# An attention and feed-forward kernel: batch 3 by casting loads, two tails earlier, one load by head pairs

## The chip, the cores and the metric

The kernel runs on one core of one Trainium2 chip. Times are microseconds (us) on the device, medians of several executions. A ratio is the mean time of one kernel's fast runs over the mean of the other kernel's fast runs of the same rounds, so it is not quite the ratio of the medians quoted beside it. The first run of the kernel before, 1282.54 us, is left out.

Engines: PE is TensorE, which multiplies matrices; DVE is VectorE; ACT is ScalarE; POOL is GpSimd; SP is SyncE, which here only issues DMAs. A name ending in q (SPq) is an engine's queue: the time that an issue took there, waits included where the queue could not go on.

## The reference

```python
# both functions are condensed
def _attn_ref(q, k, v):                  # 8 batches, 8 heads, 576 rows, 64 columns, float32
    scores = (1 / np.sqrt(D)) * np.matmul(q, k.transpose(0, 1, 3, 2))
    scores = np.where(block_i >= block_j, scores, -1e9)      # blocks of 64 rows, causal
    attn = np.exp(scores - scores.max(-1, keepdims=True))
    attn = attn / (attn.sum(-1, keepdims=True) + 1e-9)
    return np.matmul(attn, v)

# x: the heads side by side, 4608 x 512; w_gate, w_val: 512 x 1536; w_out: 1536 x 512
def _moe_ref(x, w_gate, w_val, w_out):
    return (np.maximum(x @ w_gate, 0) * (x @ w_val)) @ w_out
```

## The kernel before

The feed-forward part works through nine tiles of 512 rows. Tile j < 8 is rows 0 to 511 of batch j; the ninth gathers the 64 last rows ("tails") of every batch. A tile is 144 products of 128x512 on PE: 96 for gate and val, 48 for the output. The attention of later batches is put between these products by hand: an event `(p, f)` runs `f` after product `p` of the tile. The attention of a batch is four rounds of two heads each (rounds 8 to 11 are batch 2, round 12 is the first of batch 3), and one tail.

```python
def round_at(p, r, av, to_xT, after=(6, 13)):
    # scores and exponentials of round r at p, products with v at av,
    # and then to_xT(r): its result, transposed, into the tile xT of its batch
    ...

def to_xT_dma(r):                                # by a DMA that SP issues
    b, hp = divmod(r, 4)
    nc.sync.dma_start_transpose(xT_of(b)[:, hp, :]..., xnats[r]...)

def to_xT_pe(r, evac):                           # by PE, used for batches 0 and 1
    ...
    for c in range(4):
        nc.tensor.transpose(br[:, 128 * c : 128 * c + 128], xnat[:, c, :], ident)
    evac(xT_of(b)[:, hp, :], br[:, 0:512])
```

Batches get to the chip in two ways. Batches 0 to 3 are loaded as float32 into a staging buffer by SP and cast by POOL, DVE or ACT. Batches 0 and 1 are then transposed by PE, batches 2 and 3 by DMAs, whose results DVE and POOL put into order ("unpermute"). Batches 4 to 7 take casting loads: POOL issues a DMA that turns float32 into bfloat16 on its way, 15 loads for a batch, and SP issues four transposes from SBUF to SBUF for q and k.

```python
def load_qkv(b, which):                          # casting loads, issued by POOL
    for t in which:
        for c in range(NCH):                     # 5 chunks of rows
            ...
            nc.gpsimd.dma_start(dst, src[b, :, 128 * c : 128 * c + n, :]...)

def dma_transposes(b):                           # four transposes, issued by SP
    ...
    for t in range(2):
        nc.sync.dma_start_transpose((qTm, kTm)[t][b % 2]..., m[t])
        nc.sync.dma_start_transpose((qTt, kTt)[t][b % 2][:, 0:4, :], tl[t])
```

qTm, kTm, qTt, kTt and v_bf exist twice and are used in turn, so batch b + 2 overwrites batch b. Each engine runs its own program in order and does not wait for PE unless a buffer makes it wait. An event's place therefore fixes only the order on each engine, not the time: POOL and SP run ahead of PE when they can.

The schedule of tile 1, which the change rewrites (... marks a cut):

```python
events = tail_at(24, 0, (40, 44)) + tail_at(116, 1, (132, 136))
for r, p in ((8, 41), (9, 58), (10, 75), (11, 92)):
    events += round_at(p, r, (p + 21, p + 25), (p + 25, to_xT_dma))
events += [
    (88, lambda: e1.pe_tails((dve, act))),
    ...
    (47, load_3),                                # batch 3, staged
    ...
    (66, lambda: mains_3(0)),                    # its casts
    (81, lambda: early[3].transpose(0)),
    (82, lambda: mains_3(4)),
    (101, lambda: early[3].transpose(1)),
    (118, lambda: early[3].transpose_tails()),
    (121, un(3, 0, (dve, pool))),                # its unpermutes
    ...
]
run(144, events)
for b in range(3, B):                            # tile b - 1
    ...
    for at, which in ((4, (0, 1)), (46, (2,))):
        events.append((at, lambda b=b, w=which: load_qkv(b + 1, w)))
    events.append((66, lambda b=b: dma_transposes(b + 1)))
    run(144 * (b - 1), events)
```

The softmax here doesn't subtract the row's maximum and nothing guards it: scores larger than these inputs give would overflow.

Of the kernel before, what the change touches and what calls it, by code (L numbers as in the profile page):

```python
# [17 lines left out]
def kernel(  # L18
# [79 lines left out]
    def new_bf():  # L98
        return [sb.tile([128, 2048], BF, name=n, bufs=2) for n in ("q_bf", "k_bf")]

    def new_bt():
        return [sb.tile([64, 512], BF, name=n, bufs=2) for n in ("q_bt", "k_bt")]
# [161 lines left out]
    def load_qkv(b, which):  # L264
        for t in which:
            src = (q, k, v)[t]
            for c in range(NCH):
                n = 128 if c < 4 else 64
                if t == 2:
                    dst = v_bf[b % 2][:n, c, :, 0:64]  # L270
                else:
                    if (b, 0) not in bfs:
                        bfs[b, 0], bfs[b, 1] = new_bf(), new_bt()
                    dst = bfs[b, 0][t][:, 512 * c : 512 * c + 512] if c < 4 else bfs[b, 1][t]
                    dst = dst.rearrange("p (h d) -> p h d", h=8)
                nc.gpsimd.dma_start(  # L276
                    dst,
                    src[b, :, 128 * c : 128 * c + n, :].rearrange("h p d -> p h d"),
                )
# [3 lines left out]
    def dma_transposes(b):  # L283
        m, tl = bfs[b, 0], bfs[b, 1]
        for t in range(2):
            nc.sync.dma_start_transpose(
                (qTm, kTm)[t][b % 2].rearrange("p c h n -> p (c h) n"),
                m[t],
            )
            nc.sync.dma_start_transpose((qTt, kTt)[t][b % 2][:, 0:4, :], tl[t])  # L290
# [27 lines left out]
    def load_w_out(i):  # L318
        return load_w(wo[i], moe_w_out, 512 * i)

    def cast_w(sts, eng):
        for dst, st in sts:
            eng(dst, st)
# [118 lines left out]
    def corners(r, zero):  # L442

        at = attnT[r % 4]
        for lo, n in ((0, 512), (896, 128)):
            two = at[64:128, :, lo : lo + 2 * n].rearrange("p g (c n) -> p g c n", c=2)
            zero(two[:, :, :, 0:64])
# [36 lines left out]
    def tail_to_xT(b, x):  # L484
        nc.sync.dma_start_transpose(xTt[:, b], x)
# [197 lines left out]
    dve, act, pool = nc.vector.tensor_copy, nc.scalar.copy, nc.gpsimd.tensor_copy  # L683
# [7 lines left out]
    with tc.manual_schedule(engines={E.PE, E.DVE, E.Activation, E.Pool, E.SP}):  # L691

        e0 = Early(0)
# [55 lines left out]
        e1, e2 = Early(1), Early(2)  # L749
# [2 lines left out]
        w_out = [load_w_out(i) for i in range(2)]  # L752
        e1.load_v(0, 4)
        w_out.append(load_w_out(2))
        e1.load_qk(4, 4)
        e1.load_v(4, 4)
        e0.load_tails((0, 1))
        e0.load_tails((2,))
        e2.load_qk(0, 4)
        e2.load_qk(4, 4)  # L760
        for g in range(2):
# [5 lines left out]
        cast_w(w_out[2][:1], pool)  # L767
        last_w = [[a[:, c : c + 1] for a in w_out[2][1]] for c in range(2)]
        cast_w(last_w[:1], pool)
        e1.cast_qk(4, 4, (pool, None))  # L770
        e1.cast_v(4, 4, pool)
        e0.cast_tails((pool, pool))
        e0.cast_v_tail(pool)
        place = [32]

        def upto(p):
# [3 lines left out]
        def run(base, events):  # L780
            for p, f in sorted(events, key=lambda e: e[0]):
                upto(base + int(p))
                f()

        def round_at(p, r, av, to_xT, after=(6, 13)):

            exps = []

            def begin():
                exps.extend(visit(r))  # L790
                exps[0]()
                exps[1]()

            return [
                (p, begin),
                (p + after[0], lambda: exps[2]()),
                (min(p + after[1], av[0] - 0.5), lambda: corners(r, zero_dve)),
                *(
                    [(av[0], lambda: both_av(r))]
                    if av[1] is None  # L800
                    else [(av[i], lambda i=i: head_av(r, i)) for i in range(2)]
                ),
                (to_xT[0], lambda: to_xT[1](r)),
            ]

        def tail_at(p, b, av):
            exps = []
            x = sb.tile([64, 512], BF, name="xtail", bufs=2)

            def begin():  # L810
                exps.extend(tail_visit(b))
                exps[0]()
                exps[1]()

            def end():
                tail_av(b, 1, x)
                tail_to_xT(b, x)

            return [
                (p, begin),  # L820
                (p + 6, lambda: exps[2]()),
                (av[0], lambda: tail_av(b, 0, x)),
                (av[1], end),
            ]
# [4 lines left out]
        early = {2: e2}  # L829

        def tails_2():
            e1.cast_tails((pool, pool))
            e1.cast_v_tail(pool)
            e2.cast_tails((pool, pool))
            e2.transpose_tails()
            e2.cast_v_tail(pool)

        def v_2():
            e2.cast_v_chunks(0, pool)
            e2.cast_v_chunks(1, pool)  # L840

        def load_3():
            e3 = early[3] = Early(3)
            e3.load_qk(0, 4)
            e3.load_tails((0, 1))
            e3.load_qk(4, 4)
            e3.load_tails((2,))
            e3.load_v_chunks(0)
            e3.load_v_chunks(1)

        def mains_3(h0):
            early[3].cast_qk(h0, 4, (pool, pool))
            if h0 == 4:
                early[3].cast_tails((pool, pool))

        def v_3():
            e3 = early[3]
            for g in range(2):
                e3.cast_v_chunks(g, pool)
            e3.cast_v_tail(pool)  # L860

        def un(b, hp, engs=(dve, dve)):
            return lambda: early[b].unpermute(hp, engs)

        def mains_2(h0):
            e2.load_v_chunks(h0 // 4)
            e2.cast_qk(h0, 4, (pool, pool))
            e2.transpose(h0 // 4)

        def load_tails():  # L870
            e1.load_tails((0, 1))
            e1.load_tails((2,))
            e2.load_tails((0, 1))
            e2.load_tails((2,))

        events = round_at(96, 4, (112, 112.1), (116, pe_xT), (6, 11))
        events += round_at(104, 5, (127, 127.1), (131, pe_xT), (6, 15))
        events += round_at(128.5, 6, (139, 140), (146, pe_xT), (4, 9))
        events += round_at(138, 7, (148, None), (153, pe_xT), (3, 8))
        events += [  # L880
            (80, lambda: e1.cast_qk(0, 4, (None, dve))),
            (93, lambda: e1.pe_mains(0, (dve, act))),
            (95, lambda: e1.pe_mains(1, (dve, act))),
            (112.05, lambda: cast_w(last_w[1:], dve)),
            (120.2, lambda: e1.cast_qk(4, 4, (None, act))),
            (123, lambda: e1.pe_mains(2, (dve, act))),
            (125, lambda: e1.pe_mains(3, (dve, act))),
            (128, lambda: mains_2(0)),
            (142, lambda: e0.pe_tails((dve, act))),
            (143, lambda: mains_2(4)),  # L890
            (143, load_tails),
        ]
        run(0, events)
        events = tail_at(24, 0, (40, 44)) + tail_at(116, 1, (132, 136))
        for r, p in ((8, 41), (9, 58), (10, 75), (11, 92)):
            events += round_at(p, r, (p + 21, p + 25), (p + 25, to_xT_dma))
        events += [
            (88, lambda: e1.pe_tails((dve, act))),
            (20, lambda: store.pop()()),
            (25, un(2, 0, (dve, pool))),  # L900
            (28, un(2, 1, (dve, pool))),
            (46, v_2),
            (47, load_3),
            (52, un(2, 2, (dve, pool))),
            (56, un(2, 3, (dve, pool))),
            (60, tails_2),
            (66, lambda: mains_3(0)),
            (81, lambda: early[3].transpose(0)),
            (82, lambda: mains_3(4)),
            (101, lambda: early[3].transpose(1)),  # L910
            (118, lambda: early[3].transpose_tails()),
            (121, un(3, 0, (dve, pool))),
            (125, un(3, 1, (dve, pool))),
            (137, v_3),
        ]
        run(144, events)
        for b in range(3, B):
            events = tail_at(120, b, (136, 140))
            if b == 3:
                events += tail_at(3, 2, (21, 25))  # L920
            for i, p in enumerate((27, 50, 73, 96) if b == 3 else (2, 32, 62, 92)):
                r = 4 * b + i
                events += round_at(p, r, (p + 20, p + 24), (p + 24, to_xT_dma))
            if b == 3:
                events.append((2, un(3, 2, (dve, pool))))
                events.append((40, un(3, 3, (dve, pool))))
            if b + 1 < B:
                for at, which in ((4, (0, 1)), (46, (2,))):
                    events.append((at, lambda b=b, w=which: load_qkv(b + 1, w)))
                events.append((66, lambda b=b: dma_transposes(b + 1)))  # L930
            run(144 * (b - 1), events)
# [30 lines left out]
```

## Time and profile before

| | before |
|---|---|
| time, median of the runs beside the changed kernel | 373.54 us |
| profiled span | 372.0 us |
| PE busy | 96% |
| DVE, ACT, POOL busy | 47%, 46%, 30% |
| longest wait of PE | 3.9 us, at tile 2's start |

The head of the page of the kernel before, with the span and the busy times of the engines:

```profile
span 372.0 us, 7467 instructions
## 1 busy us (share of the span) xinstructions
PE 357.1 (96%) x2963; PEld 176.8 (48%) x2963; DVE 173.4 (47%) x399; ACT 169.5 (46%) x278; POOL 112.9 (30%) x142
```

PE is the limit. What can still be won is its idle time, which the list of PE's waits names (the three longest; total us, number, longest):

```profile
PE ffnp L568 <- DMA xT<-xnat: 3.9, 1, 3.9
PE ffnp L679 <- POOL ident masks.py:199: 1.6, 1, 1.6
PE ffnp L238 <- ACT k_bf L168: 1.6, 1, 1.6
```

L568 is a gate or val product: tile 2's fourth product waits for the xT transpose of round 11, the last of batch 2. L238 is the transposing of batch 1's k on PE, which waits for ACT's cast. The timeline of PE around the first wait (start, us, operation; what ended the idle time stands in brackets):

```profile
109.96 0.38 PE L568 MATMUL ffnp<-xT,wg 128*128 128x512 bf16 x1 [3.91 <-DMA xT<-xnat]
110.18 1.29 PE L568 MATMUL ffnp<-xT,wv 128*128 128x512 bf16 x4
111.26 1.91 PE L568 MATMUL ffnp<-xT,wg 128*128 128x512 bf16 x4
112.97 1.64 PE L568 MATMUL ffnp<-xT,wv 128*128 128x512 bf16 x4
114.45 1.03 PE L568 MATMUL ffnp<-xT,wg 128*128 128x512 bf16 x4
```

A group of four products usually starts 0.86 us after the one before it. After the wait a group takes 1.71 us: the clock is at half. The 13 products from 109.96 to 114.45 took 4.5 us instead of 2.8, so the wait costs 3.9 + 1.7 = 5.6 us. This is what the Trainium skill describes ("TensorE: Matmul & The Clock Gate", Part 1): PE's clock is halved after an idle window of about 3.4 us and comes back after a window as long of work. The trace's clock record agrees with one half-clock stretch of 3.4 us here.

POOL's timeline shows the casting loads of batch 4 and 5 (four lines of it; x4 and x5 are numbers of loads):

```profile
110.87 3.65 POOL L276 DMA_DIRECT2D q_bf<-in_q_dram  x4
120.32 4.54 POOL L276 DMA_DIRECT2D v_bf<-in_v_dram  x5
124.84 3.52 POOL L276 DMA_DIRECT2D q_bf<-in_q_dram  x4
132.47 0.77 POOL L276 DMA_DIRECT2D k_bt<-in_k_dram  x1
```

SP's timeline shows batch 4's four transposes, and behind them the xT transposes:

```profile
127.77 4.88 SPq L286 DMA_TRANSPOSE qTm<-q_bf  x1
132.75 1.26 SPq L290 DMA_TRANSPOSE qTt<-q_bt  x1
134.19 6.70 SPq L286 DMA_TRANSPOSE kTm<-k_bf  x1
140.98 1.20 SPq L290 DMA_TRANSPOSE kTt<-k_bt  x1
142.28 4.62 SPq L543 DMA_TRANSPOSE xT<-xnat  x3
```

Read together: 25 loads leave POOL as one train, and the four transposes issued into it hold SP for 14.4 us (127.8 to 142.2). Batch 5's four, issued from 168.7 us on, when the last of the loads ahead of them was landing (at 169.1 us), took 7.5.

### The profile page before, as it was taken

What the parts mean: (1) busy time and instruction counts of PE and PEld (TensorE: products, weight loads), DVE (VectorE), ACT (ScalarE), POOL (GpSimd) and SP (SyncE); (2) the same over time, 40 slices, a digit from 0 to 9 for tenths busy, and PEclk for the clock granted to TensorE, in tenths of its full rate; (3) what the DMA queues carried; (4) which work ended last, traced back from release to release, by engine and by line L of the source; (5) the groups of instructions that cost most, each with busy time, mean ns of one, the idle gap of its engine ahead of it and who ended that gap; (6) DMA issues with size and microseconds to landing.
All of it is one profiled execution on the core that took longest, in us unless ns stands there. A gap on an engine that the chain in (4) does not pass through costs nothing.

```text
span 372.0 us, 7467 instructions
## 1 busy us (share of the span) xinstructions
PE 357.1 (96%) x2963; PEld 176.8 (48%) x2963; DVE 173.4 (47%) x399; ACT 169.5 (46%) x278; POOL 112.9 (30%) x142
## 2 busy tenths in 40 slices
PE   6899979999959999999999999999999999999996
PEld 2544545544534545444554455444544454444443
DVE  4754465675513553454345543554354543323432
ACT  4833736667234663456435544553465323302310
POOL 5756644385079930750067004000000000000000
PEclk9999999999998999999999999999999999999999
DMA  8999999989889999998499846956210120020014
GB/s 252 289 348 359 306 250 319 206 209 248 132 157 115 126 143 204 116 129 149 114 89 140 123 120 82 62 74 140 79 17 14 52 92 7 0 86 28 0 34 109
DMA packets 145187, 51.35 MB, mean 138 GB/s; under 512 B 124544, under 2 KB 139136, under 8 KB 145152
## 3 DMA queue, kind: packets, MB, share of 16 engines
q1 hardware_dynamic: 83616, 34.62, 43.5%
q0 software_dynamic: 56256, 7.08, 38.6%
q10 hardware_dynamic: 5280, 9.18, 7.7%
q8 instruction: 23, 0.38, 0.5%
q14 instruction: 12, 0.10, 0.1%
HBM read 37.75 MB, written 9.44 MB: 127 GB/s over the span
## 4 chain that ended last, share of the span: by engine, by line
PE 83%; DMA 13%; SPq 1%; ACT 1%; POOL 0%; issue 0%; DVE 0%; ACTq 0%; POOLq 0%
PE ffnp L568 45%; PE ffnp L625 24%; DMA stage<-in_moe_w_gate_dram 5%; PE ffnp L491 4%; DMA stage<-in_k_dram 3%; PE sc L378 3%; PE ffnp L471 3%; DMA stage<-in_moe_w_out_dram 2%; PE one L378 1%; DMA xT<-xnat 1%; SPq L139 1%; DMA stage<-in_v_dram 1%; PE sc L412 1%; PE one L412 0%; ACT gate_sb L578 0%
## 5 line engine op out<-in xcount | busy, mean ns | idle before, releaser
L583 DVE TENSOR_TENSOR hT<-gate_sb,ffnp 128x512 bf16<-128x512 bf16 x106 | 72.8, 687 | 97.5 <-PE ffnp L568 83.2
L578 ACT ACTIVATE gate_sb<-ffnp 128x512 bf16<-128x512 f32 x108 | 64.8, 601 | 106.6 <-PE ffnp L568 103.1
L568 PE MATMUL ffnp<-xT,wg 128*128 128x512 bf16 x384 | 104.3, 382 | 4.8 <-DMA xT<-xnat 3.9
L625 PE MATMUL ffnp<-wo,hT 128*128 128x512 bf16 (+1 forms) x444 | 102.1, 374 | 0.2 <-DVE ob L645 0.2
L568 PE MATMUL ffnp<-xT,wv 128*128 128x512 bf16 x376 | 101.4, 382 | 0.0
L568 PEld LDWEIGHTS <-wv 128*128 128x128 bf16 x432 | 40.1, 98 | 50.3 <-issue 7.4
L568 PEld LDWEIGHTS <-wg 128*128 128x128 bf16 x432 | 40.3, 98 | 48.3 <-issue 5.6
L625 PEld LDWEIGHTS <-hT 128*128 128x128 bf16 x444 | 40.6, 98 | 41.5 <-issue 1.1
L387 ACT ACTIVATE attnT<-sc 128x1024 bf16<-128x1024 f32 x56 | 57.0, 1039 | 0.2 <-issue 0.2
L659 DVE COPY ob<-ffnp 128x512 f32<-128x512 f32 (+1 forms) x35 | 23.7, 677 | 39.1 <-PE ffnp L625 39.1
L276 POOL DMA_DIRECT2D v_bf<-in_v_dram x20 | 17.1, 883 | 69.5 <-PE ffnp L471 69.5
L491 PEld LDWEIGHTS <-attnT 128*128 128x128 bf16 x640 | 26.2, 98 | 13.9 <-DVE xnat L457 3.5
L456 DVE RECIPROCAL recip<-ffnp 128x4 f32<-128x4 f32 (+1 forms) x73 | 13.1, 179 | 33.1 <-PE ffnp L491 21.3
L491 PE MATMUL ffnp<-v_bf,attnT 128*128 128x65 bf16 x570 | 26.4, 194 | 0.0
L393 ACT ACTIVATE attnT<-one 128x256 bf16<-128x256 f32 x28 | 10.7, 383 | 33.1 <-PE ffnp L378 28.3
L457 DVE TENSOR_TENSOR xnat<-ffnp,recip 128x256 bf16<-128x256 f32 x57 | 24.2, 425 | 2.6 <-DMA xT<-xnat 0.7
L433 ACT ACTIVATE attnTt<-one 64x256 bf16<-64x256 f32 x8 | 3.0, 378 | 33.5 <-PE ffnp L412 33.5
L378 PE MATMUL sc<-qTm,kTm 64*128 64x512 bf16 (+1 forms) x168 | 17.4, 305 | 0.0
L378 PEld LDWEIGHTS <-kTm 64*128 64x128 bf16 x224 | 9.6, 94 | 15.0 <-issue 10.7
L424 ACT ACTIVATE attnTt<-sc 128x1024 bf16<-128x1024 f32 x16 | 15.6, 1014 | 0.0
L223 POOL COPY kTm<-perm 128x512 bf16<-128x512 bf16 x8 | 9.7, 1231 | 19.1 <-DMA perm<-k_bf 14.1
L276 POOL DMA_DIRECT2D k_bf<-in_k_dram x16 | 14.3, 953 | 0.0
(87 smaller groups left out, 262.6 us busy)
## 6 DMA issues: line engine op xcount, KB each, us to landing
out_dram<-ob ACTq DMA_DIRECT2D x32, 256.0 KB, 2.5
stage<-in_moe_w_gate_dram SPq DMA_DIRECT2D x6, 512.0 KB, 9.0
stage<-in_moe_w_val_dram SPq DMA_DIRECT2D x6, 512.0 KB, 8.8
stage<-in_q_dram SPq DMA_DIRECT2D x6, 512.0 KB, 6.4
stage<-in_k_dram SPq DMA_DIRECT2D x6, 512.0 KB, 7.5
stage<-in_moe_w_out_dram SPq DMA_DIRECT2D x6, 512.0 KB, 8.5
stage<-in_v_dram SPq DMA_DIRECT2D x20, 128.0 KB, 5.3
stage<-in_v_dram SPq DMA_DIRECT2D x8, 256.0 KB, 6.5
```

Source lines behind the costliest of these rows:

```text
L276: nc.gpsimd.dma_start(dst, src[b, :, 128 * c : 128 * c + n, :].rearrange("h p d -> p h d"),)
L378: nc.tensor.matmul(where[c].rearrange("p (c n) -> p c n", n=128), kTm[b % 2][head_of(hh), c, hp, :], qTm[b % 2][head_of(hh), c:4, hp, :], ...
L387: return lambda: nc.scalar.activation(at[:, :, lo : lo + 512], sc, AF.Exp, scale=scale)
L424: return lambda: nc.scalar.activation(at[:, :, 2 * i : 2 * i + 2, 0:256], main[i].rearrange("p g (h n) -> p g h n", h=2), AF.Exp, scale=scale,
L456: nc.vector.reciprocal(recip, av[:, :, 64])
L457: nc.vector.tensor_tensor(out=out, in0=av[:, :, 0:64], in1=recip.to_broadcast([rows, n, 64]), op=AX.mult,)
L491: nc.tensor.matmul(av[:, p, :], at[:, col : col + 128], v_bf[b % 2][:, c, h, :], start=(p == 0), stop=(c == p), skip_group_check=True,)
L568: nc.tensor.matmul(to, (wg, wv)[t][f // 4][:, c, 128 * (f % 4) : 128 * (f % 4) + 128], x[:, c], start=(c == 0), stop=(c == 3),)
L578: nc.scalar.activation(gate_sb, gate, AF.Relu)
L583: nc.vector.tensor_tensor(out=h, in0=gate_sb, in1=val, op=AX.mult)
L625: nc.tensor.matmul(op, hT[f][:, 128 * s : 128 * (s + 1)], wo[f // 4][:, f % 4, n0:n1], start=(f == lo), stop=(f == hi - 1),)
L659: nc.vector.tensor_copy(ob, op)
```

## The change

The intent: load batch 3 like the later batches, which spares POOL's casts and the unpermutes on DVE and POOL. For that batch 1's buffers must be free earlier, so both tails of batches 0 and 1 go ahead of batch 2's rounds. The second half of batch 1's q and k is loaded and cast two heads at a time, so that PE gets the first pair sooner.

The diff, cut to its core (... marks cuts; what is left out is the removed `load_3`, `mains_3`, `v_3`, the places where batch 1's tails were loaded and cast before and the casts by POOL that go with the moved loads, and batch 2's third unpermute, now at 50 instead of 52):

```diff
-        e1.load_qk(4, 4)
+        for h0 in (4, 6):
+            e1.load_qk(h0, 2)
         e1.load_v(4, 4)
-        e0.load_tails((0, 1))
-        e0.load_tails((2,))
+        for e in (e0, e1):
+            e.load_tails((0, 1))
+            e.load_tails((2,))
         e2.load_qk(0, 4)
 ...
-        events += round_at(128.5, 6, (139, 140), (146, pe_xT), (4, 9))
+        events += round_at(126, 6, (138.2, 139), (146, pe_xT), (4, 9))
 ...
-            (120.2, lambda: e1.cast_qk(4, 4, (None, act))),
+            (119, lambda: e1.cast_qk(4, 2, (None, act))),
+            (120.2, lambda: e1.cast_qk(6, 2, (None, act))),
             (123, lambda: e1.pe_mains(2, (dve, act))),
-            (125, lambda: e1.pe_mains(3, (dve, act))),
+            (129, lambda: e1.pe_mains(3, (dve, act))),
 ...
+            (142, lambda: e1.pe_tails((dve, act))),
 ...
-        events = tail_at(24, 0, (40, 44)) + tail_at(116, 1, (132, 136))
-        for r, p in ((8, 41), (9, 58), (10, 75), (11, 92)):
-            events += round_at(p, r, (p + 21, p + 25), (p + 25, to_xT_dma))
+        events = tail_at(24, 0, (37, 39)) + tail_at(40, 1, (55, 58))
+        for r, p in ((8, 54), (9, 67), (10, 80), (11, 94)):
+            events += round_at(p, r, (p + 21, p + 24), (p + 24, to_xT_dma))
         events += [
-            (88, lambda: e1.pe_tails((dve, act))),
 ...
-            (47, load_3),
-            (60, tails_2),
-            (66, lambda: mains_3(0)),
-            ... (transposes, casts and unpermutes of batch 3)
+            (59, lambda: load_qkv(3, (0, 1))),
+            (90, tails_2),
+            (92, lambda: load_qkv(3, (2,))),
+            (105, lambda: dma_transposes(3)),
         ]
```

At 105 batch 3's four transposes enter SP's queue, and round 11's xT follows at 94 + 24 = 118.

More of the change, by code (lines that the diff above doesn't have):

```diff
@@ L769 @@
         cast_w(last_w[:1], pool)
-        e1.cast_qk(4, 4, (pool, None))
+        for h0 in (4, 6):
+            e1.cast_qk(h0, 2, (pool, None))
         e1.cast_v(4, 4, pool)
-        e0.cast_tails((pool, pool))
-        e0.cast_v_tail(pool)
+        for e in (e0, e1):
+            e.cast_tails((pool, pool))
+            e.cast_v_tail(pool)
         place = [32]
@@ L831, in tails_2 @@
         def tails_2():
-            e1.cast_tails((pool, pool))
-            e1.cast_v_tail(pool)
             e2.cast_tails((pool, pool))
@@ L840, in v_2 @@
             e2.cast_v_chunks(1, pool)
-        def load_3():
-            e3 = early[3] = Early(3)
-            e3.load_qk(0, 4)
-            e3.load_tails((0, 1))
-            e3.load_qk(4, 4)
-            e3.load_tails((2,))
-            e3.load_v_chunks(0)
-            e3.load_v_chunks(1)
-        def mains_3(h0):
-            early[3].cast_qk(h0, 4, (pool, pool))
-            if h0 == 4:
-                early[3].cast_tails((pool, pool))
-        def v_3():
-            e3 = early[3]
-            for g in range(2):
-                e3.cast_v_chunks(g, pool)
-            e3.cast_v_tail(pool)
         def un(b, hp, engs=(dve, dve)):
@@ L870, in load_tails @@
         def load_tails():
-            e1.load_tails((0, 1))
-            e1.load_tails((2,))
             e2.load_tails((0, 1))
@@ L902 @@
             (46, v_2),
-            (47, load_3),
-            (52, un(2, 2, (dve, pool))),
+            (50, un(2, 2, (dve, pool))),
             (56, un(2, 3, (dve, pool))),
-            (60, tails_2),
-            (66, lambda: mains_3(0)),
-            (81, lambda: early[3].transpose(0)),
-            (82, lambda: mains_3(4)),
-            (101, lambda: early[3].transpose(1)),
-            (118, lambda: early[3].transpose_tails()),
-            (121, un(3, 0, (dve, pool))),
-            (125, un(3, 1, (dve, pool))),
-            (137, v_3),
+            (59, lambda: load_qkv(3, (0, 1))),
+            (90, tails_2),
+            (92, lambda: load_qkv(3, (2,))),
+            (105, lambda: dma_transposes(3)),
         ]
@@ L923 @@
                 events += round_at(p, r, (p + 20, p + 24), (p + 24, to_xT_dma))
-            if b == 3:
-                events.append((2, un(3, 2, (dve, pool))))
-                events.append((40, un(3, 3, (dve, pool))))
             if b + 1 < B:
```

## The prediction

> **What bounds the kernel now.** TensorE: busy 357.1 of 372.0 us (busy times of the page). In stretches of 10 us it is busy 10.00 from 110 to 360 us, so only the first third has time to give. PE's waits name it: 3.9 us at 105.8 us, where tile 2's first product waits for batch 2's last xT transpose; 1.6 us at 50.3 us, for the ScalarE cast of batch 1's k; start-up. After the 3.9 us wait, eight matmuls start 0.43 instead of 0.216 us apart, 1.7 us more; the clock record shows half clock for 3.4 us, as the Trainium skill says ("TensorE: Matmul & The Clock Gate", Part 1: half rate after an idle window of about 3.4 us). So this boundary costs 5.6 us.
>
> **What the change does.** PE gets the same work in another order. Removed: batch 3's unpermutes (DVE 0.6, GpSimd about 1.2 us each), GpSimd casts (about 1 us each) and staged loads. DVE and GpSimd are 47% and 30% busy: off the critical path, worth nothing directly.
>
> - *Head pairs.* k of heads 4, 5 lands about 1.5 us before all of k, and its cast is half of 1.05 us. The 1.6 us wait should mostly go. Estimate: -1.3 us.
> - *Tails earlier.* Needed so that batch 3 can overwrite batch 1's buffers. They leave only some 26 matmuls, 6 us, between round 11's transpose (position 118) and tile 2.
> - *Batch 3 by casting loads.* GpSimd takes 0.9 us for each issue and runs ahead: q, k, v of batch 3 and q, k of batch 4 go out as one train of 25 loads. The kernel before has just this train for batches 4 and 5: 110.9 to 133.2 us, the last landing 146.6. The four transposes issued inside it took 14.4 us on SP (127.8 to 142.2; 7.5 us at 168.7, without loads), and the xT transpose behind them landed at 148.3. The skill ("DMA: Bandwidth & Descriptors", Queues, rings and completion order) says why: each DMA engine takes packets from its queues in turn. The DMA share of 2.2 there agrees.
>
> The train should now start when GpSimd is done with batch 2's unpermutes, near 77 us. Batch 3's transposes start near 95.5 us, and **round 11's xT waits behind them on SP**: it lands at 106 us (uncongested) to 115 us (as in the train). PE wants it at about 103 us; before, PE resumed at 109.9. So the wait is not removed: it moves and probably grows, half clock after it included.
>
> **Prediction.** Resumption shifts by -3.5 us (uncongested) to +5 us, weighted to the second; from there PE is packed as before. 377 us, 370 to 383 in 8 of 10. Faster by over 2%: 0.06; within 2%: 0.79; slower by over 2%: 0.15.
>
> **What would show it.** PE's waits: that for the cast of k under 0.6 us; that for xT still the largest, 3 to 12 us, at 102 to 115 us. SP's queue: batch 3's four transposes just ahead of round 11's xT, 7 to 14 us in all. GpSimd: casting loads from about 77 us in one train. Granted clock: half for about 3.4 us after the wait. Windows after that: PE 10.00.
>
> **What would make it wrong.** Transposes done before round 11's product (up to 7 us gained); batch 4's loads held back; a new wait in rounds 8 to 11, now 13 instead of 17 matmuls apart.

## The result

The changed kernel took 384.24 us (383.83 to 384.79, 4 runs) against 373.54 us; the ratio is 1.0298, with a 95% interval of 1.0259 to 1.0336. It is slower by 3%, outside the predicted range of 370 to 383 us.

The head of its page:

```profile
span 382.3 us, 7410 instructions
## 1 busy us (share of the span) xinstructions
PE 354.3 (93%) x2915; PEld 176.5 (46%) x2963; DVE 170.1 (44%) x395; ACT 169.3 (44%) x279; POOL 112.6 (29%) x145
```

The list of PE's waits (the longest, and two that are new):

```profile
PE ffnp L568 <- DMA xT<-xnat: 12.8, 1, 12.8
PE ffnp L625 <- POOL wo L323: 1.5, 1, 1.5
PE ffnp L471 <- DVE hT L583: 1.2, 1, 1.2
```

The same product waits for the same transpose, 12.8 us instead of 3.9. PE's timeline behind it (four lines of it):

```profile
119.78 0.58 PE L568 MATMUL ffnp<-xT,wg 128*128 128x512 bf16 x1 [12.76 <-DMA xT<-xnat]
121.86 1.91 PE L568 MATMUL ffnp<-xT,wg 128*128 128x512 bf16 x4
123.57 1.34 PE L568 MATMUL ffnp<-xT,wv 128*128 128x512 bf16 x4
124.74 1.03 PE L568 MATMUL ffnp<-xT,wg 128*128 128x512 bf16 x4
```

PE goes on at 119.8 us, 9.8 us later than before (109.96). The 13 products to 124.74 (one has no record in the trace) take 5.0 us, 2.2 more than at full clock; before, it was 1.7 more. The later start and the 0.5 us more of half clock sum to 10.3 us, which is the whole difference of the two spans. From there on the lists of waits show nothing of note in either trace.

SP's timeline says why xT is late:

```profile
92.82 5.51 SPq L543 DMA_TRANSPOSE xT<-xnat  x2
98.52 6.71 SPq L286 DMA_TRANSPOSE qTm<-q_bf  x1
105.33 1.23 SPq L290 DMA_TRANSPOSE qTt<-q_bt  x1
106.73 5.93 SPq L286 DMA_TRANSPOSE kTm<-k_bf  x1
112.76 1.21 SPq L290 DMA_TRANSPOSE kTt<-k_bt  x1
114.06 1.22 SPq L543 DMA_TRANSPOSE xT<-xnat  x1
```

Round 11's products with v were done at about 100 us, but SP issued its transpose only at 114.1, when batch 3's four were through: 15.5 us for these (98.5 to 114.0). It landed 5.7 us after its issue. SP did not wait for data of batch 3 here: the last load of its q and k, issued at 88.4 us, had landed by 93.9 us. The four went out right behind round 10's xT, and for that SP had to wait until DVE had made round 10's result from PE's products:

```profile
96.69 0.42 DVE L457 TENSOR_TENSOR xnat<-ffnp,recip 128x256 bf16<-128x256 f32 x1
97.14 1.19 SPq L543 DMA_TRANSPOSE xT<-xnat  x1
```

So PE's own pace set when the four entered the queue. And POOL's timeline shows the train around them (four lines of it):

```profile
80.46 3.86 POOL L276 DMA_DIRECT2D q_bf<-in_q_dram  x4
90.80 4.24 POOL L276 DMA_DIRECT2D v_bf<-in_v_dram  x5
94.95 3.60 POOL L276 DMA_DIRECT2D q_bf<-in_q_dram  x4
103.09 0.69 POOL L276 DMA_DIRECT2D k_bt<-in_k_dram  x1 [0.36 <-issue]
```

The q of batch 3 leaves at 80.5 us; that of batch 4, which no one needs before tile 3, leaves at 95.0, just ahead of the transposes.

### The profile page after: what moved, and what is told of

It is laid out like the page before. It is cut to its first block, busy times and chain, and to the rows that moved or that the text cites. A ratio compares the mean times of both kernels' runs of the same rounds, so it can differ in the third digit from the quotient of the medians.

```text
span 382.3 us, 7410 instructions
## 1 busy us (share of the span) xinstructions
PE 354.3 (93%) x2915; PEld 176.5 (46%) x2963; DVE 170.1 (44%) x395; ACT 169.3 (44%) x279; POOL 112.6 (29%) x145
## 4 chain that ended last, share of the span: by engine, by line
PE 76%; DMA 14%; SPq 6%; issue 1%; POOL 1%; DVE 1%; POOLq 0%
PE ffnp L568 42%; PE ffnp L625 22%; DMA stage<-in_moe_w_gate_dram 5%; PE ffnp L491 4%; SPq L139 4%; PE sc L378 3%; PE ffnp L471 3%; DMA stage<-in_v_dram 2%; DMA stage<-in_k_dram 2%; DMA perm<-q_bf 2%; SPq L286 2%; DMA xT<-xnat 1%; PE one L378 1%; DMA stage<-in_q_dram 1%; SPq L158 1%
## 5 line engine op out<-in xcount | busy, mean ns | idle before, releaser
L568 PE MATMUL ffnp<-xT,wg 128*128 128x512 bf16 x367 | 101.5, 383 | 14.4 <-DMA xT<-xnat 12.8
L625 PE MATMUL ffnp<-wo,hT 128*128 128x512 bf16 (+1 forms) x421 | 98.2, 373 | 3.0 <-POOL wo L323 1.5
L276 POOL DMA_DIRECT2D v_bf<-in_v_dram x25 | 21.0, 866 | 96.7 <-PE ffnp L471 96.7
L276 POOL DMA_DIRECT2D q_bf<-in_q_dram x20 | 18.1, 947 | 0.0
L276 POOL DMA_DIRECT2D k_bf<-in_k_dram x20 | 17.9, 954 | 0.0
L378 PEld LDWEIGHTS <-kTm 64*128 64x128 bf16 x224 | 9.5, 94 | 15.5 <-issue 11.3
```

The costliest lines, as they stand in the source:

```text
L378: nc.tensor.matmul(where[c].rearrange("p (c n) -> p c n", n=128), kTm[b % 2][head_of(hh), c, hp, :], qTm[b % 2][head_of(hh), c:4, hp, :], ...
L568: nc.tensor.matmul(to, (wg, wv)[t][f // 4][:, c, 128 * (f % 4) : 128 * (f % 4) + 128], x[:, c], start=(c == 0), stop=(c == 3),)
L625: nc.tensor.matmul(op, hT[f][:, 128 * s : 128 * (s + 1)], wo[f // 4][:, f % 4, n0:n1], start=(f == lo), stop=(f == hi - 1),)
```

## The experiments

Two theories were set against each other. **Q**: the order on SP holds xT back, since it stands behind the transposes of batch 3. **T**: the train of casting loads makes every transpose slow, whatever the order. A third possibility had to be kept open: that the earlier tails and the denser rounds cost time themselves. The runs came in three groups, each on one chip with its own runs of the kernel before (medians 374.39, 373.85 and 374.10 us). All results were correct.

| run | edit, on which kernel | us | ratio to before | 95% interval |
|---|---|---|---|---|
| a_swap | xT of round 11 ahead of batch 3's transposes, changed | 379.49 | 1.0154 | 1.0091 to 1.0218 |
| a_hold4 | batch 4's loads held back, changed | 375.54 | 1.0043 | 0.9984 to 1.0101 |
| a_pe11 | xT of round 11 by PE, changed | 377.61 | 1.0080 | 1.0005 to 1.0155 |
| b_pe11 | xT of round 11 by PE, before | 373.22 | 0.9961 | 0.9895 to 1.0027 |
| a_pe11_gates | both cures, changed | 370.02 | 0.9907 | 0.9859 to 0.9955 |
| b_pe11_gates | both cures, before | 370.77 | 0.9912 | 0.9874 to 0.9950 |
| c_order | the change without its casting loads | 374.30 | 1.0011 | 0.9961 to 1.0062 |
| a_junk | 54 idle products in the wait, changed | 382.66 | 1.0225 | 1.0171 to 1.0279 |
| a_same | the changed kernel again | 385.11 | 1.0292 | 1.0263 to 1.0322 |
| a_late_tails | batch 1's tails behind batch 2, changed | 382.94 | 1.0242 | 1.0205 to 1.0279 |
| a_junk66 | 66 idle products in the wait, changed | 383.67 | 1.0271 | 1.0238 to 1.0305 |
| b_pairs | the head pairs alone, before | 374.56 | 1.0007 | 0.9981 to 1.0032 |

### a_swap: the other order on SP

```diff
-            (105, lambda: dma_transposes(3)),
+            (119, lambda: dma_transposes(3)),
```

> The changed kernel with batch 3's four transposes issued behind round 11's xT transpose on SP instead of ahead of it. Theory Q (the order on SP holds xT back): xT is issued near 101 us and lands by about 108 us instead of 119.7; PE's wait for it falls from 12.8 to 0 to 1.5 us. Batch 3's own transposes then start 4 us later and land near 122 us, so round 12 (27 matmuls into tile 2) should wait some 6 us: total 377 to 380. Rival theory T (the train of casting loads alone makes xT slow, whatever the order): xT still lands near 119 us and the total stays at 383 to 385.

The list of PE's waits of this run:

```profile
PE one L378 <- DMA kTm<-k_bf: 5.1, 1, 5.1
PE ffnp L568 <- DMA xT<-xnat: 3.1, 1, 3.1
```

The wait for xT fell from 12.8 to 3.1 us, so the order on SP is a cause. It did not fall to 1.5: issued at about 100.6 us, xT still needed 9.3 us to land (PE went on at 109.9), because the train was under way. Both theories hold a part. The four transposes, now later, let round 12 wait 5.1 us for kTm: about half of what the one wait lost, the next one took. The total was 379.49 us.

### a_hold4: batch 4's loads held back

POOL copies one column of tile 2's xT before it issues batch 4's loads. A real read of the data makes it wait, so no race arises. The order on SP is as in the changed kernel.

```diff
+    gate = consts.tile([128, 1], BF, name="gate")
 ...
+                if b == 3:      # ahead of load_qkv(4) in the events of tile 2
+                    events.insert(
+                        0, (4, lambda: nc.gpsimd.tensor_copy(gate, xT_of(2)[:, 3, 0:1])))
```

> The changed kernel with batch 4's casting loads held back: GpSimd first copies one column of tile 2's xT, so they start only when round 11's xT has landed. The order on SP is unchanged. Theory T (the second half of the train makes the four transposes slow): they take 7 to 9 us on SP instead of 15.5, xT lands at 109 to 112 us, PE waits 2 to 5 us, total 374 to 377. Theory Q in its pure form (only the order matters, the train does not): xT lands near 119 us as before, total 383 to 385.

SP's timeline (without the line of qTt), and under it two lines of POOL's, of this run:

```profile
97.87 3.82 SPq L287 DMA_TRANSPOSE qTm<-q_bf  x1
103.16 3.35 SPq L287 DMA_TRANSPOSE kTm<-k_bf  x1
106.62 1.19 SPq L291 DMA_TRANSPOSE kTt<-k_bt  x1
107.90 1.22 SPq L544 DMA_TRANSPOSE xT<-xnat  x1
```

```profile
90.11 4.24 POOL L277 DMA_DIRECT2D v_bf<-in_v_dram  x5
110.39 0.19 POOL L906 COPY gate<-xT 128x1 bf16<-128x1 bf16 x1 [16.04 <-DMA xT<-xnat]
```

The four transposes took 9.9 us instead of 15.5, a little more than expected; batch 3's v was still landing until 100.8 us. xT stood behind them as ever and landed in time for PE to go on at 110.4. The wait was 4.0 us, the total 375.54 us. So pure Q falls: with the order unchanged, taking half of the train away wins back nearly all. The loss needs both, a queue in order and a train that slows what stands ahead in it. By what means the loads slow a transpose inside the DMA engines, no run here isolates.

### a_pe11 and b_pe11: no DMA at the boundary

Round 11's result is transposed by PE, as it is for batches 0 and 1 (for the kernel before, 25 and 31 in place of 24 and 30).

```diff
-            events += round_at(p, r, (p + 21, p + 24), (p + 24, to_xT_dma))
+            to_xT = (p + 24, to_xT_dma) if r < 11 else (p + 30, lambda r: to_xT_pe(r, act))
+            events += round_at(p, r, (p + 21, p + 24), to_xT)
```

> The changed kernel with round 11's xT made by four TensorE transposes and a ScalarE copy, so nothing at the boundary waits for a DMA. Theory Q and T both: the 12.8 us wait is gone. Batch 3's transposes still land at 119 us, so round 12, which PE reaches near 115.5 us, should wait about 4 us: total 374 to 377. If the lost time is elsewhere (the earlier tails, the denser rounds), the total stays above 380.

> The kernel before with the same edit. Its wait of 3.9 us for xT and the 1.7 us of half clock behind it should go, 0.3 us of transposes come: 368 to 369.5 us, 0.985 to 0.989 of before. If the half clock is not caused by the wait, only 3.6 us are won: 370 us.

The longest wait of each, a_pe11 first:

```profile
PE one L378 <- DMA kTm<-k_bf: 6.3, 1, 6.3
```

```profile
PE ffnp L568 <- DMA xT<-xnat: 3.5, 2, 2.5
```

In the changed kernel the wait at the boundary is gone, and round 12 waits 6.3 us for batch 3's kTm instead: 4 us were expected. In the kernel before the boundary is clear as well, but the expected 368 to 369.5 us did not come. The trace shows two new waits for xT, 1.0 and 2.5 us, at 147 to 151 us, at the start of tile 3. PE arrived there earlier, while batch 3's xT transposes stood behind batch 4's four in the train of that time: the one that ended the longer wait was issued 5.1 us earlier than before, at 140.6, and yet landed at 151.2 us, as before (151.1). The gain was taken back one boundary later, by the same mechanism.

### a_pe11_gates and b_pe11_gates: both cures

To the edit above, for every batch from 3 on, a copy that holds back the next batch's loads until the last transpose of this batch has landed:

```diff
+                events.insert(
+                    0, (4, lambda b=b: nc.gpsimd.tensor_copy(gate, kTt[b % 2][:, 0, 0:1])))
```

> The changed kernel with round 11's xT made by TensorE, and from batch 4 on each batch's casting loads held back on GpSimd until the last transpose of the batch before has landed (a copy of one column of kTt). Theory (order on SP and the train of loads together make the whole loss): no wait for xT, and round 12's wait for kTm, 6.3 us with the TensorE transposes alone, goes as well, because batch 3's transposes now land near 109 us; the next boundary stays clear too. PE packed from 20 us on but for 2 to 4 us of small waits: 369 to 371.5 us, 0.985 to 0.992 of before. Rival (the denser rounds or the earlier tails cost by themselves): 375 or more.

> The kernel before with the same two edits. With the TensorE transposes alone it had no wait at tile 2, but 3.5 us of waits for xT at tile 3, behind batch 4's transposes inside the train of loads. If the train is the cause of these too, holding batch 5's loads back removes them and the half clock after them: 367.5 to 370 us, 0.980 to 0.988 of before. If not, the 3.5 us stay: 372 to 374.

The page's line of the granted clock in 40 slices of the span, in tenths, first of the changed kernel, then of a_pe11_gates:

```profile
PEclk9999999999975999999999999999999999999999
```

```profile
PEclk9999999999999999999999999999999999999999
```

What is left of the wait for xT in a_pe11_gates is this line of PE's waits:

```profile
PE ffnp L569 <- DMA xT<-xnat: 0.6, 1, 0.6
```

With both cures the changed kernel ran in 370.02 us and the kernel before in 370.77 us (its longest wait for xT is 1.3 us). Both beat the kernel before by 0.9%, with intervals that leave out 1, and the two cannot be told apart. Of the third possibility, that the tails and rounds themselves cost, nothing is left. The second half of this result is that the change has no merit of its own that these runs could see: with the same cures in both kernels, what it takes from DVE and POOL won nothing above the noise (each interval is about 0.5% to either side).

### c_order: the change without its casting loads

The changed kernel with `load_3`, `mains_3`, `v_3` and batch 3's transposes and unpermutes put back at their old places.

> The change without its casting loads: head pairs, both tails early and the denser rounds as in the changed kernel, batch 3 staged, cast and unpermuted as before. If the loss comes from the casting loads of batch 3 (their transposes on SP and the train), this runs like the kernel before, 372 to 377 us, with a wait for xT of 2 to 6 us near 105 us. If the earlier tails and denser rounds cost by themselves, 380 or more.

```profile
PE ffnp L568 <- DMA xT<-xnat: 3.6, 1, 3.6
```

With the new order and the old way of loading, the wait is 3.6 us and the time that of the kernel before, 374.30 us. The earlier tails, the denser rounds and the head pairs cost nothing together that shows (the interval is 0.5% to either side); the casting loads of batch 3 carry the loss.

### a_junk and a_junk66: what the half clock costs

Products of zeros at the end of tile 1, into a buffer that no one reads, so that PE isn't idle in the wait. Their number is 54, then 66.

```diff
+            (143, lambda: junk(54)),
```

> The changed kernel with 54 idle products (128x512, 11.6 us) on TensorE at the end of tile 1, inside the wait for xT, so that TensorE isn't idle there. xT still lands near 119.7 us. If the half clock comes from the idle time, the record shows full clock around the boundary and about 2 us are won: 381.5 to 382.5. If it costs nothing or doesn't come from the idle time: 384.

> As the run with 54 idle products, but with 66, so that they reach to the landing of xT (14.2 us from 105 us on): with 54, 1.9 us of idle time were left and half clock followed for 3.4 us all the same. If idle time brings the half clock, however short: full clock around the boundary now, and 1.5 to 2.2 us are won against the changed kernel on this chip, 0.5 us lost where the products run past the landing. If idle products don't count as work: half clock stays and nothing is won.

With 54 the idle products ended too early: 1.9 us of idle time were left, and the clock was at half afterwards for 3.4 us all the same. The 13 products behind the wait took 4.5 us, against 5.0 in the changed kernel. The median was 382.66 us; since the changed kernel itself did not run on that chip, no gain is read from it. With 66 there was no wait, and PE's timeline shows full speed right away:

```profile
120.77 1.03 PE L568 MATMUL ffnp<-xT,wv 128*128 128x512 bf16 x4
121.63 1.03 PE L568 MATMUL ffnp<-xT,wg 128*128 128x512 bf16 x4
```

The time was 383.67 against 385.11 us of the changed kernel on the same chip, 1.4 us less, where 1.5 to 2.2, less 0.5 for the products that ran past the landing, was expected. But the two sets of four runs overlap (383.42 to 385.91, and 383.96 to 385.61 us), and so do the intervals, so the gain in time is not shown. What the trace shows is that the half clock behind the boundary went when the idle time went; idle products are no cure for the rest.

### a_same and a_late_tails: why the train left late

The prediction had the loads start at 77 us, when POOL would be done with batch 2's unpermutes; they started at 80.5. In the kernel before, the last two of these unpermutes began at 77.3 us and ended at 79.8, so 77 asked for a gain of 2.8 us that the prediction gave no ground for. In the changed kernel batch 1's tail loads stand ahead of batch 2's q and k, and batch 2's first transpose landed at 71.1 us instead of 67.9, and POOL's unpermutes, which come ahead of the casting loads, wait for it.

```diff
-        for e in (e0, e1):
-            e.load_tails((0, 1))
-            e.load_tails((2,))
+        e0.load_tails((0, 1))
+        e0.load_tails((2,))
         e2.load_qk(0, 4)
         e2.load_qk(4, 4)
+        e1.load_tails((0, 1))
+        e1.load_tails((2,))
 ...      (their casts behind batch 2's, at 143; PE's transposes at 36 of tile 1)
```

> The changed kernel as it is, once more, as the yardstick for the next two on the same chip: 383 to 385 us, wait for xT 12 to 14 us.

> The changed kernel with batch 1's tails loaded, cast and transposed behind batch 2's q and k instead of ahead of them (TensorE transposes them at 36 of tile 1). In the changed kernel batch 2's first transpose landed at 71.1 us, 3.3 us later than before, GpSimd's casting loads started at 80.5 instead of the 77 predicted, and PE had a new wait of 1.2 us for a DVE multiply held up by batch 2's unpermute. If the three tail loads are the cause: that transpose lands near 68.5, the loads start at 77 to 78.5, the 1.2 us wait goes, xT lands at 116 to 118, total 380.5 to 382.5. If the head pairs or something else are the cause: loads start at 80 to 81, total 383 to 385.

The changed kernel repeated its result: 385.11 us, 14.2 us of wait, loads from 80.4 us. With the tails later that transpose landed at 68.5 us, the loads started at 78.8 us, PE's wait for the DVE multiply was gone (it was 1.2 us in the first profile, 0.3 in the repetition), and the time was 382.94 us, 2.2 less than the repetition; the two intervals overlap a little. The start of the loads moved by half of the 3.5 us in question; the other half is not explained by the tail loads. The wait itself did not become shorter. It moved, as the lines of PE that end it show, the repetition first:

```profile
121.01 0.58 PE L568 MATMUL ffnp<-xT,wg 128*128 128x512 bf16 x1 [14.22 <-DMA xT<-xnat]
119.24 0.59 PE L568 MATMUL ffnp<-xT,wg 128*128 128x512 bf16 x1 [14.07 <-DMA xT<-xnat]
```

PE came to the boundary 1.6 us earlier, SP issued round 10's xT 1.6 us earlier (95.3 instead of 96.9) and batch 3's transposes right behind it, and PE went on 1.8 us earlier. The loads had moved by as much, so this run alone does not part their share from PE's.

### b_pairs: the head pairs alone

The pair loads, the pair casts and the moved places of round 6 and of the transposes, from the diff above, on the kernel before.

> The kernel before with the head pairs alone (loads, casts, the second half's transposes, round 6 two products earlier). By the prediction the 1.6 us wait for the cast of k goes: 1.3 us won, ratio 0.996 to 0.998. By what the changed kernel showed (k no longer waited for, but 1.5 us for the cast of the last piece of w_out, which landed 1.3 us later), the wait only moves: ratio 0.998 to 1.002, with a wait of 1 to 1.5 us for w_out or k in the profile.

The ratio is 1.0007 with an interval of 0.9981 to 1.0032: no gain. In its profile there was neither the wait for k nor one over 0.3 us for w_out, so the expected move of the wait to w_out, which the changed kernel's first profile shows (1.5 us), is not regular. PE's wait for xT at the boundary was still 3.7 us, but it ended at 108.6 us instead of 110.0: in the profiled execution, the fastest of the six (372.89 us), the pairs' time was won and kept. Why the six together show no gain stays open.

## Why the prediction was wrong

- **Right: PE's idle time decides, and what is taken from DVE and POOL is worth nothing.** No run contradicts it; the two cured kernels, 370.02 and 370.77 us, agree with it within their noise.
- **Right: the mechanism.** Round 11's xT stood behind batch 3's four transposes on SP, inside one train of 25 loads; the wait for it stayed the longest, half clock followed, and PE was packed from there on (the windows after 130 us show 9.79 to 10.00 of 10 where 10.00 was predicted, but this trace lacks 48 of the 2963 matmul records). a_swap and a_hold4 showed each half of it: either the order or the train undone brings the wait from 12.8 to 3 or 4 us.
- **Wrong: the steps "Batch 3's transposes start near 95.5 us" and "it lands at 106 us (uncongested) to 115 us (as in the train)".** It landed at 119.7, and PE went on 9.8 us later than before where the prediction allowed +5 at most. This is a term of the sum that was mis-sized, in three places. The transposes started at 98.5 instead of 95.5 us (+3.0). The prediction puts this start beside that of the loads and gives no other ground for it, and the loads were late as well (80.5 instead of 77 us). But batch 3's q and k had landed by 93.9 us; SP came to the transposes only behind round 10's xT, whose data PE and DVE had ready at 97.1 us. So this term is the lateness of PE, passed on by the order on SP one round earlier. The four transposes took 15.5 instead of 14.4 us (+1.1). The xT then landed 5.7 us after its issue, about the 6.0 of the train before (-0.3). The rest, 0.9 us, is rounding of the 115 us, which the sum of these terms (95.5 + 14.4 + 6.0) had really put at 115.9.
- **Wrong: weighting towards the middle.** The lower end, 106 us, assumed transposes without loads beside them. Nothing in the schedule held batch 4's loads back, so there was no ground for it, and it pulled the 377 us down.
- **Wrong: the head pairs' -1.3 us.** The wait for k went, as predicted, but b_pairs won nothing.
- **Too small: the half clock.** It cost 2.2 instead of 1.7 us: the clock record has half clock until 124.2 us, 4.4 us after PE went on, where 3.4 us were predicted. In a_junk66, with the wait filled, it was gone.
- **Wrong: "PE wants it at about 103 us".** It wanted it at 107.0, with new waits of 1.5 us for w_out and 1.2 us for a DVE multiply behind batch 2's late unpermute. This did not only change the length of the wait: by the first term above, PE's lateness also put off the moment at which it ended, and a_late_tails shows the two moving together.

## What to carry to other kernels

Before a bulk load is moved or changed in kind, look at what stands in the same queue behind the transfers that depend on it: a transfer that PE waits for next must not queue behind one that is needed a tile later. An engine that runs ahead will issue the load after next as well, and its traffic slows what is urgent; a cheap read of data that lands at the right moment holds it back without a race. When one wait is cured, look at the next boundary before counting the gain: b_pe11 lost its gain there, and a_pe11 lost part of its own already at the next round of attention.

## What the Trainium skill lacked or had wrong

- "DMA: Bandwidth & Descriptors", Issuing engines are not separate DMA queues, says that DMAs of all issuers share the 16 DMA engines and interleave. The traces agree, but it gives no figure for what this does to a DMA transpose: the issue of one 128x2048 transpose held SP for 1.9 us when the loads ahead of it had all but landed (the kernel before, at 168.7 us) and for 6.7 us among casting loads (the changed kernel); the four of a batch took 7.5 and 15.5 us.
- The same page, Anatomy of one DMA, calls the generating of descriptors small, with many of them before its cost shows. Here each casting load of 128 KB kept GpSimd busy for 0.9 us, and 25 of them took 23.3 us (80.46 to 103.78, with 1.7 us of casts among them). Only that row misleads: the same page, Latency and other measured facts, puts the first byte on this path at about 1 us and names GpSimd's writing of descriptors as the reason, and 0.9 us is close to it.
- "TensorE: Matmul & The Clock Gate", Part 1, gives an idle window of about 3.4 us ahead of half clock. In a_junk the clock was at half for 3.4 us after only 1.9 us of idle time, with 0.7 us of small products just ahead of it. Apart from those that the end of the run cuts off, the half-clock stretches in the records are 3.4 us or a multiple of it, which fits the page's window.
